# The opening of a fused Mamba-2 and expert-merge kernel: first decays in eight rows, a new order of loads, copies and products, and two stores on another queue

## The chip, the cores and the metric

The kernel runs on one core of one Trainium2 chip. The metric is device time in microseconds (us) of one execution. The five engines are TensorE (PE), VectorE (DVE), ScalarE (ACT), GpSimd (POOL) and SyncE (SP, which issues transfers). Each engine takes its instructions in the order in which the program gives them; between engines, semaphores make one wait for another. ACT and POOL can issue transfers too, and then the transfer stands in that engine's order.

## What is computed

First a Mamba-2 scan over 4 sequences of 768 steps, 8 heads, head width 32, state width 16. Then a merge of four expert networks over the 3072 tokens of width 256:

```python
la  = np.log(np.clip(a, 1e-06, 1.0))          # decays, per head and step
cum = np.cumsum(la, axis=-1)                  # inside a chunk
L   = np.exp(cum[:, :, :, None] - cum[:, :, None, :]) * causal
y   = (C B^T * L) x  +  (C state) * exp(cum)  # inside the chunk, and carried in
state = exp(sum la) * state + sum_j B_j x_j exp(cum_end - cum_j)

p = probs / (probs.sum(-1, keepdims=True) + 1e-09)
for e in range(4):
    out += p[:, e:e + 1] * (np.maximum(y @ w1[e], 0.0) @ w2[e])
```

All of it is in 32-bit floats. The two products with w1 (256 x 1024) and w2 (1024 x 256) for each expert are nearly all of the work.

## The kernel before

The 3072 tokens are 24 chunks of 128. The scan is done in 12 steps ("p") of two half chunks of 64, four sequences at once; the merge is done in four blocks of six chunks, with weights in pieces of 256 columns (`fb`), and with sums of pieces formed beforehand so that fewer products are needed. Two kinds of order occur.

The opening is written out by hand, lines 560 to 784. It loads the first decays, heads and tokens, makes the first step of the scan, and prepares what all later steps use. Everything after it is put in order by a planner (`Plan`, lines 69 to 273). It keeps a clock for each engine, gives every operation a home for its result and an engine where there is a choice (sums of weights or of token values may go to VectorE or GpSimd), and starts from two numbers, `now, START = 9.6, 11.0`: the times, in its own units, at which VectorE is free and PE begins the long run of products. Its order is fixed when the program is built.

In the opening these names matter:

- `a_q`, `a_q2`: the decays of step 0 (and 1), and of step 2, each 4 groups of heads by 2 halves of sequences. They lie in a tile of 128 rows, of which only eight hold data: row 32q + s, for group q and half s. The other rows are zero-filled first (lines 566, 567, 586), since the product that follows reads 32 rows of each group. `load_a` brings the data, `ready` clips it and zeroes the first column, and `spread` copies one row to 64 rows of a bank by a product with `own`, a 0/1 column: for each group q two products of 32 rows by 64 columns, one for each half s, in different corners of the array.
- `scan` (line 507) forms on VectorE the running products of the decays in `MT[0]`, for one group q of heads from `four[q]`, a bank of PSUM.
- `pr`, the expert probabilities; three small GpSimd sums make `total_p` (lines 623 to 626), VectorE takes its reciprocal, GpSimd forms `pc`, PE transposes it (`turn_gates`), ScalarE keeps it as `p_sb`, and `spread_gate` spreads the first expert's row to all rows, for `gate`.
- `mask` and `score`: heads B and C, masked by ScalarE and multiplied by PE into `seven`, four banks, in two halves s of the sequences.
- `end_of(q)`: a small GpSimd copy of the last columns of `MT[0]`, made before `masked(q)` (VectorE) or `aside(q)` (ScalarE and GpSimd, for q = 2) multiplies the scores into `MT[0]` in place. `F` is formed from these copies on GpSimd.
- `inner`: 64 small products of `MT[0]` with the tokens. Their result is copied to `yT0`, the first tokens of the merge. `state` makes the first state.
- `a_sb` (also called `cum`): all decays, loaded at once; clipped, logarithm on ScalarE, transposed (`turn_logs`), summed (`sum_logs`, `minus_logs`), and stored in memory (`cum_d`, `cumh_d`), from where later steps read them again (`ah`, `ab`). `p_d` holds the gates in the same way.
- `idle`: products of ones, whose result nobody reads, that keep PE running.

The loads go out on two queues. SP: half of the first decays, half of the heads, half of the tokens, all decays, two pieces of w1, the decays of step 2, two pieces of w1, the tokens of step 1, four pieces of w2. ACT: the probabilities, then the other halves. Eight transfers can be under way; the ninth waits for the landing of the first, and so on.

At the end, six pieces of the output are turned by PE, copied by VectorE or ScalarE, and stored by `send`, each by one transfer from SP and one from ACT (line 1395).

Of the kernel before, what the change touches and what calls it, by code (L numbers as in the profile page):

```python
# [8 lines left out]
FP32 = mybir.dt.float32  # L9
AF = mybir.ActivationFunctionType  # L10
ALU = mybir.AluOpType

P = 128
# [346 lines left out]
def kernel(  # L360
# [198 lines left out]

    a_q, a_q2 = (homes["V"][-i].rearrange("p c (t x) -> p c t x", t=NT) for i in (1, 4))  # L560

# [22 lines left out]
    tmask = const.tile([P, NT], FP32)  # L584
    nc.vector.memset(tmask, 0.0)
    nc.vector.memset(a_q2, 0.0)
    for fb in range(2):
        load_w1(fb, homes["W"][fb])
    for s in range(2):
        load_a(1, s, a_q2, nc.sync)  # L590
    for fb in range(2, 4):
        load_w1(fb, homes["W"][fb])
    for c in range(2):
        load_tokens(1, c, xt[1][:])
    for fb in range(4):
        load_w2(fb, homes["W"][4 + fb])

    ident = const.tile([P, P], FP32)
    make_identity(nc, ident)
# [19 lines left out]

    ready(a_q, 0)  # L620

# [14 lines left out]

    def turn_gates(banks):
        for z in range(NSEQ):
            nc.tensor.transpose(
                banks[z // 2][:rows, FB + z % 2 * P:FB + z % 2 * P + P],  # L640
                pc[:, z].rearrange("p e k -> p (e k)"), ident)
        for i in range(2):
            nc.scalar.copy(
                out=p_sb[:, :, 2 * i:2 * i + 2].rearrange("p e z i -> p z e i"),
                in_=banks[i][:rows, FB:].rearrange("p (z e i) -> p z e i", z=2, e=2))

    def spread_gate(bank, gate):
        nc.tensor.matmul(  # L648
            out=bank[:, FB:], lhsT=ident[:rows, 0:1].to_broadcast([rows, P]),
            rhs=p_sb[:, 0].rearrange("p z i -> p (z i)"), start=True, stop=True,  # L650
            skip_group_check=True)
        nc.scalar.copy(
            out=gate[:, :2].rearrange("p c x -> p (c x)"), in_=bank[:, FB:])

    def spread(a_q, e, banks, half, order=range(NQ)):
        for q in order:
            for s in range(2):
                k = slice(32 * q, 32 * q + 32)
                nc.tensor.matmul(  # L659
                    out=banks[q][HALF * s:HALF * s + HALF, FB * half:FB * half + FB].rearrange(  # L660
                        "p (x i) -> p x i", x=4),
                    lhsT=own[k, s].to_broadcast([32, HALF]),
                    rhs=a_q.rearrange("p c t x -> p (c t) x")[k, :, HALF * e:HALF * e + HALF],
                    start=True, stop=True, tile_position=(32 * q, HALF * s), skip_group_check=True)

# [27 lines left out]
    def turn_logs(bank):  # L693
        nc.scalar.activation(out=a_sb, in_=a_sb, func=AF.Ln)
# [45 lines left out]
    for i, q in enumerate(ORDER):  # L740
        scan(0, q, MT[0], four[q], 0)
        if not i:
            nc.vector.reciprocal(total_p, total_p)
    nc.gpsimd.tensor_mul(
        pc.rearrange("p z e k -> p z k e"), pr.rearrange("p (z k) e -> p z k e", z=NSEQ),
        total_p.rearrange("p (z k) e -> p z k e", z=NSEQ).to_broadcast([P, NSEQ, NC, E]))
    turn_gates(As)
    for s in range(2):
# [27 lines left out]
    sum_logs(As[0])  # L776
    nc.sync.dma_start(out=p_d, in_=p_sb)
    state(F[0], xt[0], As, 0, True)
    spread(a_q2, 0, four, 0, ORDER)
    minus_logs(ys[0])  # L780
    keep_state(homes["A"][0], As, 0)
    bound = const.tile([P, HALF], FP32)
# [7 lines left out]
    B512, B256 = {"DVE": D512, "POOL": 1.3}, {"DVE": D256, "POOL": .72}  # L790
    now, START = 9.6, 11.0

# [20 lines left out]
    yT[0, 0] = plan.taken("V", NV - 3, START)  # L813
    for i in (0, NV - 4, NV - 1):
        plan.homes["V"][i].free = now
# [560 lines left out]
    def last(k, groups):  # L1376
# [16 lines left out]
        def send(d, n, r, to):  # L1393
            for c, (queue, on_) in enumerate(((nc.sync, "SP"), (nc.scalar, "ACT"))):
                plan.add({on_: ISSUE}, lambda e, c=c, queue=queue: queue.dma_start(
                    out=dst[d, 3 * k + n, c][:, to],
                    in_=r.t[HALF * c:HALF * c + HALF, 0, to.start * P:to.stop * P].rearrange(
                        "p (s m) -> p s m", m=P)), lag=LANDING + .2, kb=32 * (to.stop - to.start),
                    reads=[r])

# [269 lines left out]
```

## Time and profile before

| what | us |
|---|---|
| three timed runs | 613.78, 614.91 (median), 617.61 |
| the profiled execution's own time | 613.47 |
| span of the profiled execution | 611.7 |
| PE busy | 600.8 (98%) |
| DVE busy | 493.8 (81%) |
| ACT busy | 276.6 (45%) |
| POOL busy | 140.4 (23%) |
| chain that ended last: share of PE | 97%, of it line 985 91% |
| first product of line 985 starts | 17.74 |

The span runs from the first instruction of the program to the last event; the own time has some 1.7 us more around it. Line 985 is the product of 128x256 of the merge (`product`). A chain of waits is followed back from the last instruction: at each step to what released it. Since PE has 97% of that chain, the time is the sum of PE's work and of the few places where PE waits or runs at a lower clock.

### The profile page before, as it was taken

To read this page: it belongs to the slowest core of one execution; us is meant where nothing else is said; L and a number is where in the kernel's file an instruction comes from. 1 tells how busy PE (TensorE), PEld (TensorE's weight loads), DVE (VectorE), ACT (ScalarE), POOL (GpSimd) and SP (SyncE) were. 2 spreads that over 40 slices of the span, in tenths; PEclk is the share of its full clock that TensorE was granted. 3 is DMA by queue.
4 is the path that set the end of the run, shared out by engine and by line. 5 is a ranking of instruction groups with operands and counts; after the bars stand their busy time and mean duration, and the time that the engine had idled before them with its cause. 6 is when DMAs were issued, how large, how long until landed. Compare 5 with 4: busy or idle time off the path is not lost.

```text
span 611.7 us, 12256 instructions
## 1 busy us (share of the span) xinstructions
PE 600.8 (98%) x4530; PEld 516.8 (84%) x4530; DVE 493.8 (81%) x851; ACT 276.6 (45%) x624; POOL 140.4 (23%) x147
## 2 busy tenths in 40 slices
PE   7999999999999999999999999999999999999997
PEld 4777888888888888888888888878888888888886
DVE  4769999999999995786988988386785989576794
ACT  3247557674542626765243343434444242434440
POOL 5662656656510000367401000000000000000000
PEclk8999999999999999999999999999999999999999
DMA  7577568878623329773432415963242322964002
GB/s 216 141 223 221 185 206 264 245 235 293 224 90 111 83 33 349 211 225 138 137 87 71 123 31 146 304 198 105 70 132 68 111 71 35 339 220 137 1 1 53
DMA packets 99856, 93.78 MB, mean 153 GB/s; under 512 B 33500, under 2 KB 69052, under 8 KB 99796
## 3 DMA queue, kind: packets, MB, share of 16 engines
q1 hardware_dynamic: 98120, 92.04, 49.3%
q10 hardware_dynamic: 1676, 0.96, 0.6%
q8 instruction: 36, 0.59, 0.4%
q14 instruction: 24, 0.20, 0.1%
HBM read 72.79 MB, written 20.17 MB: 152 GB/s over the span
## 4 chain that ended last, share of the span: by engine, by line
PE 97%; DMA 1%; issue 0%; SPq 0%; DVE 0%; POOL 0%; ACT 0%; DVEq 0%; POOLq 0%
PE bank L985 91%; PE bank L532 2%; PE bank L499 1%; PE bank L918 1%; DMA cum<-in_a_dram 1%; PE bank L541 1%; PE bank L1455 0%; PE bank L1391 0%; PE bank L659 0%; SPq L442 0%; PE bank L648 0%; PE bank L685 0%; DVE bank L1143 0%; DVE v L1020 0%; SPq L447 0%
## 5 line engine op out<-in xcount | busy, mean ns | idle before, releaser
L985 PE MATMUL bank<-v,w 128*128 128x256 f32 x1876 | 435.1, 380 | 1.6 <-issue 0.8
L985 PEld LDWEIGHTS bank<-v,w 128*128 128x128 f32 x1876 | 354.7, 190 | 52.6 <-issue 1.7
L985 PE MATMUL bank<-Y,w 128*128 128x256 f32 x692 | 177.1, 380 | 0.0
L1012 DVE TENSOR_TENSOR v<-v,v 128x512 f32<-128x512 f32 x238 | 175.1, 757 | 1.7
L1285 ACT COPY v<-bank 128x512 f32<-128x512 f32 x120 | 70.4, 587 | 202.7 <-PE bank L985 199.0
L985 PEld LDWEIGHTS bank<-Y,w 128*128 128x128 f32 x692 | 130.6, 190 | 19.4 <-ACT v L994 0.9
L1020 DVE SCALAR_TENSOR_TENSOR v<-bank,gate 128x512 f32<-128x512 f32 x162 | 111.1, 686 | 42.4 <-PE bank L985 37.9
L1045 POOL TENSOR_TENSOR w<-w,w 128x512 f32<-128x512 f32 (+1 forms) x84 | 95.6, 1151 | 102.9 <-DVE v L1012 31.1
L999 ACT COPY bank<-v 128x512 f32<-128x512 f32 x141 | 81.6, 593 | 19.7 <-DVE v L1020 14.2
L1143 DVE TENSOR_TENSOR bank<-bank,v 128x512 f32<-128x512 f32 x92 | 62.6, 693 | 33.3 <-PE bank L985 22.8
L994 ACT COPY v<-bank 128x512 f32<-128x512 f32 x111 | 65.2, 587 | 53.2 <-PE bank L985 45.1
L515 ACT ACTIVATE MT<-ab,neg 128x64 f32<-128x64 f32 x144 | 37.4, 338 | 0.0
L1012 DVE TENSOR_TENSOR v<-bank,v 128x512 f32<-128x512 f32 x30 | 20.6, 686 | 9.3 <-PE bank L985 6.5
L1321 DVE TENSOR_TENSOR v<-v,v 128x256 f32<-128x256 f32 x65 | 24.5, 415 | 1.0 <-ACT v L1285 0.7
L1020 DVE SCALAR_TENSOR_TENSOR v<-v,gate 128x512 f32<-128x512 f32 x30 | 24.1, 804 | 0.4
L880 POOL TENSOR_TENSOR cts<-ctm,dec 128x512 f32<-128x512 f32 x11 | 14.0, 1270 | 36.0 <-DVE Y L1115 24.2
L937 ACT COPY v<-bank 64x256 f32<-64x256 f32 (+1 forms) x33 | 12.3, 373 | 20.1 <-PE bank L541 15.8
L1012 POOL TENSOR_TENSOR v<-v,v 128x512 f32<-128x512 f32 x12 | 15.2, 1270 | 16.4 <-DVE v L1012 10.0
L682 DVE TENSOR_TENSOR MT<-bank,MT 128x256 f32<-128x256 f32 x47 | 16.6, 411 | 2.4 <-POOL ends L673 2.4
L520 DVE TENSOR_TENSOR MT<-MT,bound 128x512 f32<-128x512 f32 x18 | 16.5, 932 | 0.0
L489 ACT ACTIVATE ctm<-bct,tmask 128x256 f32<-128x256 f32 (+1 forms) x26 | 11.3, 485 | 6.3 <-DMA bct<-in_xbc_dram 6.3
L532 PEld LDWEIGHTS bank<-MT,xt 64*32 64x32 f32 x768 | 9.8, 110 | 2.4 <-issue 2.0
(95 smaller groups left out, 180.9 us busy)
## 6 DMA issues: line engine op xcount, KB each, us to landing
w<-w_d SPq DMA_DIRECT2D x128, 256.0 KB
w<-in_w_dram SPq DMA_DIRECT2D x72, 256.0 KB
w_d<-w SPq DMA_DIRECT2D x64, 256.0 KB
gate<-p_d SPq DMA_DIRECT2D x15, 384.0 KB
ab<-cum_d SPq DMA_DIRECT2D x36, 128.0 KB
xt<-in_xbc_dram SPq DMA_DIRECT2D x46, 96.0 KB
bct<-in_xbc_dram SPq DMA_DIRECT2D x5, 512.0 KB
out_dram<-v SPq DMA_DIRECT2D x144, 16.0 KB
```

The costliest lines, as they stand in the source:

```text
L515: nc.scalar.activation(out=MT[:, q, c, t], in_=ab[:, c, h], func=AF.Exp, bias=neg[:, e, t, i:i + 1])
L532: nc.tensor.matmul(out=y[to:to + 32], lhsT=xt[k, c, h:h + D], rhs=MT[k, q, c, t], start=start, stop=True, tile_position=(HALF * s, to), sk ...
L682: nc.vector.tensor_mul(v, bank[:, FB * half:FB * half + FB], v)
L985: nc.tensor.matmul(out=o, lhsT=w[:, j], rhs=x if half is None else x[:, j], start=(start and j == 0), stop=(j == 1), skip_group_check=True)
L994: act(.5, lambda e: nc.scalar.copy(out=flat(v), in_=bank.t), reads=[bank], writes=[v])
L999: act(.54 if to - lo > FB else .32, lambda e: nc.scalar.copy(out=bank.t[:, lo:to], in_=flat(v)[:, lo:to]), reads=[v], writes=[bank])
L1012: plan.add(engines, lambda e: (on(e).tensor_add if sign > 0 else on(e).tensor_sub)(flat(v), whole(x), whole(y)), reads=[x, y], writes=[v], ...
L1020: dve(D512, lambda e: nc.vector.scalar_tensor_tensor(out=h.t, in0=whole(x).rearrange("p (j m) -> p j m", j=JJ), scalar=0.0, in1=g.t[:, 2 * ...
L1045: (on(e).tensor_add if sign > 0 else on(e).tensor_sub)(out, x, y)
L1143: dve(D512, lambda e: (nc.vector.tensor_add if sign > 0 else nc.vector.tensor_sub)(to.t, bank.t, whole(x)), reads=[x, bank], writes=[to])
L1285: act(.5, lambda e: nc.scalar.copy(out=flat(v), in_=bank.t), reads=[bank], writes=[v], hold=HOLD)
L1321: plan.add(engines, lambda e: (on(e).tensor_add if sign > 0 else on(e).tensor_sub)(o[1](), x[1](), y[1]()), reads=[v for v in vs if v is n ...
```

## The change

The first decays now lie in rows 0 to 7 of their tile (row 4s + q), and nothing is filled with zeros. `own` becomes a table of 8 rows, with a 0/1 block for each group, in a free tile, and `spread` is one product of 8 rows by 128 columns for each group. Both halves of `a_q` are made ready at once. The loads are ordered anew: the probabilities go out on ACT after the decays and the heads, all tokens go on SP, the decays of step 2 on ACT, and of w2 two pieces only; the other two follow the stores of the sums. GpSimd's copies `ends` come before its other work, two of them ahead of `pc`; the clip of `a_sb` goes to VectorE after the masks, its logarithm to ScalarE after that. `turn_gates` writes one bank and stands between the two halves of the scores. Of the second spread of `a_q`, two groups stand after the scores and two after `inner`; `spread_gate` uses a bank of `four`; `state` moves ahead of the sums of logs. One `idle` of 256 columns becomes one of 128, and two of 128 go. The planner starts from 9.2 and 10.8, and one more tile is held until `now`. The two stores of output piece (0, 0) go out from GpSimd.

```diff
-    a_q, a_q2 = (homes["V"][-i].rearrange("p c (t x) -> p c t x", t=NT) for i in (1, 4))
+    ROWS = 2 * NQ
+    a_q, a_q2 = (homes["V"][-i][:ROWS].rearrange("p c (t x) -> p c t x", t=NT) for i in (1, 4))
...
-    nc.vector.memset(a_q[:, 0], 0.0)
-    nc.gpsimd.memset(a_q[:, 1], 0.0)
-    nc.scalar.dma_start(out=pr, in_=probs)
...
-            out=a_q.rearrange("(q r) c t x -> q r c (t x)", q=NQ)[:, s], in_=a_rows[k, s])
+            out=a_q[NQ * s:NQ * s + NQ].rearrange("q c t x -> q c (t x)"), in_=a_rows[k, s])
     for s, queue in enumerate((nc.sync, nc.scalar)):
         load_a(0, s, a_q, queue)
-    load_heads(0, bct[0], slice(0, 2))
-    load_heads(0, bct[0], slice(2, 4), nc.scalar)
-    load_tokens(0, 0, xt[0][:])
-    load_tokens(0, 1, xt[0][:], nc.scalar)
+        load_heads(0, bct[0], slice(2 * s, 2 * s + 2), queue)
+    nc.scalar.dma_start(out=pr, in_=probs)
     nc.scalar.preload_act_table_set("natural_log_exp_and_others")
+    for c in range(2):
+        load_tokens(0, c, xt[0][:])
+    for s in range(2):
+        load_a(1, s, a_q2, nc.scalar)
...
-    nc.vector.memset(a_q2, 0.0)
-    for fb in range(2):
-        load_w1(fb, homes["W"][fb])
-    for s in range(2):
-        load_a(1, s, a_q2, nc.sync)
-    for fb in range(2, 4):
+    for fb in range(4):
         load_w1(fb, homes["W"][fb])
...
-    for fb in range(4):
+    for fb in range(2):
         load_w2(fb, homes["W"][4 + fb])
...
-    own = const.tile([P, 2, 1], FP32)
-    nc.vector.reduce_sum(
-        own, ident.rearrange("p (q r) -> p r q", r=32)[:, 0:2], axis=mybir.AxisListType.X)
+    own = homes["V"][-5][:ROWS].rearrange("p a (q s j) -> p (a q) s j", s=2, j=HALF)
+    nc.vector.tensor_copy(
+        out=own, in_=ident[:ROWS, :ROWS].rearrange("p (s q) -> p q s", s=2).unsqueeze(3).to_broadcast(
+            [ROWS, NQ, 2, HALF]))
...
-    ready(a_q, 0)
+    for e in range(2):
+        ready(a_q, e)
...
+    def spread(a_q, e, banks, half, order):
         for q in order:
...
+            nc.tensor.matmul(
+                out=banks[q][:, FB * half:FB * half + FB].rearrange("p (x i) -> p x i", x=4),
+                lhsT=own[:, q].rearrange("p s j -> p (s j)"),
+                rhs=a_q.rearrange("p c t x -> p (c t) x")[:, :, HALF * e:HALF * e + HALF],
+                start=True, stop=True, skip_group_check=True)
...
     idle(BANK[6], 0, 4)
-    idle(BANK[7], 0, 2)
+    idle(BANK[7], 0, 1)
     spread(a_q, 0, four, 0, ORDER)
-    idle(BANK[7], 0, 1)
     idle(BANK[7], 0, 1)
...
-        if not i:
+        if q == 3:
             nc.vector.reciprocal(total_p, total_p)
+    for q in ORDER[:2]:
+        end_of(q)
     nc.gpsimd.tensor_mul(
...
-    turn_gates(As)
-    for s in range(2):
-        score(0, ctm[0], bct[0], seven, 0, s)
-    clip(nc.gpsimd, a_sb)
-    for q in ORDER:
+    for q in ORDER[2:]:
         end_of(q)
+    score(0, ctm[0], bct[0], seven, 0, 0)
+    turn_gates(four[2])
+    score(0, ctm[0], bct[0], seven, 0, 1)
     aside(2, seven[2])
+    keep_gates(four[2])
+    spread(a_q, 1, four, 1, (3, 0))
     for q in (3, 0, 1):
         masked(q, MT[0], seven[q])
-    spread_gate(ys[1], homes["gate"][0])
-    idle(four[0], 2, 3)
-    ready(a_q, 1)
+    clip(nc.vector, a_sb)
+    nc.scalar.activation(out=a_sb, in_=a_sb, func=AF.Ln)
+    spread_gate(four[2], homes["gate"][0])
...
-    turn_logs(As[1])
+    spread(a_q, 1, four, 1, (1, 2))
...
-    spread(a_q, 1, four, 1, ORDER)
-    sum_logs(As[0])
-    nc.sync.dma_start(out=p_d, in_=p_sb)
     state(F[0], xt[0], As, 0, True)
+    turn_logs(As[1])
     spread(a_q2, 0, four, 0, ORDER)
-    minus_logs(ys[0])
+    sum_logs(As[0])
+    nc.sync.dma_start(out=p_d, in_=p_sb)
+    for fb in range(2, 4):
+        load_w2(fb, homes["W"][4 + fb])
     keep_state(homes["A"][0], As, 0)
+    minus_logs(ys[0])
...
-    now, START = 9.6, 11.0
+    now, START = 9.2, 10.8
...
-            for c, (queue, on_) in enumerate(((nc.sync, "SP"), (nc.scalar, "ACT"))):
+            by = ((nc.sync, "SP"), (nc.scalar, "ACT")) if (d, n) != (0, 0) else ((nc.gpsimd, "POOL"),) * 2
+            for c, (queue, on_) in enumerate(by):
```

In this diff `keep_gates` is the second half of the old `turn_gates`: one copy of 24x512 from the bank to `p_sb` on ScalarE.

More of the change, by code (lines that the diff above doesn't have):

```diff
@@ L572, in load_a @@
         queue.dma_start(
-            out=a_q.rearrange("(q r) c t x -> q r c (t x)", q=NQ)[:, s], in_=a_rows[k, s])
+            out=a_q[NQ * s:NQ * s + NQ].rearrange("q c t x -> q c (t x)"), in_=a_rows[k, s])
     for s, queue in enumerate((nc.sync, nc.scalar)):
         load_a(0, s, a_q, queue)
-    load_heads(0, bct[0], slice(0, 2))
-    load_heads(0, bct[0], slice(2, 4), nc.scalar)
-    load_tokens(0, 0, xt[0][:])
-    load_tokens(0, 1, xt[0][:], nc.scalar)
+        load_heads(0, bct[0], slice(2 * s, 2 * s + 2), queue)
+    nc.scalar.dma_start(out=pr, in_=probs)
     nc.scalar.preload_act_table_set("natural_log_exp_and_others")
+    for c in range(2):
+        load_tokens(0, c, xt[0][:])
+    for s in range(2):
+        load_a(1, s, a_q2, nc.scalar)
     nc.sync.dma_start(
         out=a_sb, in_=a.rearrange("c h s -> (c h) s").rearrange("(p r) s -> p r s", r=2))
-    tmask = const.tile([P, NT], FP32)
-    nc.vector.memset(tmask, 0.0)
-    nc.vector.memset(a_q2, 0.0)
-    for fb in range(2):
-        load_w1(fb, homes["W"][fb])
-    for s in range(2):
-        load_a(1, s, a_q2, nc.sync)
-    for fb in range(2, 4):
+    for fb in range(4):
         load_w1(fb, homes["W"][fb])
@@ L594 @@
         load_tokens(1, c, xt[1][:])
-    for fb in range(4):
+    for fb in range(2):
         load_w2(fb, homes["W"][4 + fb])
+    tmask = const.tile([P, NT], FP32)
+    nc.vector.memset(tmask, 0.0)
     ident = const.tile([P, P], FP32)
@@ L635, with turn_gates, keep_gates @@
     p_sb = homes["V"][0][:rows].rearrange("p e (z i) -> p e z i", z=NSEQ)
-    def turn_gates(banks):
+    def turn_gates(bank):
         for z in range(NSEQ):
             nc.tensor.transpose(
[L640 to L645, printed above, removed]
+                bank[:rows, z * P:z * P + P], pc[:, z].rearrange("p e k -> p (e k)"), ident)
+    def keep_gates(bank):
+        nc.scalar.copy(
+            out=p_sb.rearrange("p e z i -> p z e i"),
+            in_=bank[:rows].rearrange("p (z e i) -> p z e i", z=NSEQ, e=2))
     def spread_gate(bank, gate):
         nc.tensor.matmul(
-            out=bank[:, FB:], lhsT=ident[:rows, 0:1].to_broadcast([rows, P]),
+            out=bank[:, :FB], lhsT=ident[:rows, 0:1].to_broadcast([rows, P]),
             rhs=p_sb[:, 0].rearrange("p z i -> p (z i)"), start=True, stop=True,
@@ L652, in spread_gate @@
         nc.scalar.copy(
-            out=gate[:, :2].rearrange("p c x -> p (c x)"), in_=bank[:, FB:])
-    def spread(a_q, e, banks, half, order=range(NQ)):
+            out=gate[:, :2].rearrange("p c x -> p (c x)"), in_=bank[:, :FB])
+    def spread(a_q, e, banks, half, order):
         for q in order:
-            for s in range(2):
[L658 to L664, printed above, removed]
+            nc.tensor.matmul(
[3 more added lines that the diff above has]
+                start=True, stop=True, skip_group_check=True)
     MT, F = homes["MT"], homes["F"]
@@ L693, in turn_logs @@
     def turn_logs(bank):
-        nc.scalar.activation(out=a_sb, in_=a_sb, func=AF.Ln)
         for t in range(NT):
@@ L739 @@
         mask(0, ctm[0], bct[0], slice(2 * s, 2 * s + 2))
-    for i, q in enumerate(ORDER):
+    for q in ORDER:
         scan(0, q, MT[0], four[q], 0)
-        if not i:
+        if q == 3:
             nc.vector.reciprocal(total_p, total_p)
+    for q in ORDER[:2]:
+        end_of(q)
     nc.gpsimd.tensor_mul(
@@ L746 @@
         total_p.rearrange("p (z k) e -> p z k e", z=NSEQ).to_broadcast([P, NSEQ, NC, E]))
-    turn_gates(As)
-    for s in range(2):
-        score(0, ctm[0], bct[0], seven, 0, s)
-    clip(nc.gpsimd, a_sb)
-    for q in ORDER:
+    for q in ORDER[2:]:
         end_of(q)
+    score(0, ctm[0], bct[0], seven, 0, 0)
+    turn_gates(four[2])
+    score(0, ctm[0], bct[0], seven, 0, 1)
     aside(2, seven[2])
+    keep_gates(four[2])
+    spread(a_q, 1, four, 1, (3, 0))
     for q in (3, 0, 1):
         masked(q, MT[0], seven[q])
-    spread_gate(ys[1], homes["gate"][0])
-    idle(four[0], 2, 3)
-    ready(a_q, 1)
+    clip(nc.vector, a_sb)
+    nc.scalar.activation(out=a_sb, in_=a_sb, func=AF.Ln)
+    spread_gate(four[2], homes["gate"][0])
     for c in range(2):
@@ L774 @@
     ready(a_q2, 0)
-    spread(a_q, 1, four, 1, ORDER)
+    state(F[0], xt[0], As, 0, True)
+    turn_logs(As[1])
+    spread(a_q2, 0, four, 0, ORDER)
     sum_logs(As[0])
     nc.sync.dma_start(out=p_d, in_=p_sb)
-    state(F[0], xt[0], As, 0, True)
-    spread(a_q2, 0, four, 0, ORDER)
+    for fb in range(2, 4):
+        load_w2(fb, homes["W"][4 + fb])
+    keep_state(homes["A"][0], As, 0)
     minus_logs(ys[0])
-    keep_state(homes["A"][0], As, 0)
     bound = const.tile([P, HALF], FP32)
@@ L813 @@
     yT[0, 0] = plan.taken("V", NV - 3, START)
-    for i in (0, NV - 4, NV - 1):
+    for i in (0, NV - 5, NV - 4, NV - 1):
         plan.homes["V"][i].free = now
@@ L1398, in send @@
                         "p (s m) -> p s m", m=P)), lag=LANDING + .2, kb=32 * (to.stop - to.start),
-                    reads=[r])
+                    reads=[r], port=False)
         def piece(d, n, x, y, sign):
```

## The prediction

> **What bounds the kernel.** I read the page first: TensorE (PE) is busy 600.8 of the 611.7 us span and the granted clock is full in all but the first of its 40 slices, so a change pays only where PE stands still or runs slowly. I then asked for busy time by stretches, and for the chain of waits in order of time. From 17.73 us, where the long run of 128x256 products (L985) begins, to 594 us PE is busy 574.66 of 576.27 us. The rest lies in the opening and in the last 10 us, and both are touched by this change.
>
> ```profile
> 4.02 4.23 DMA cum<-in_a_dram
> ...
> 8.33 0.48 POOL cum L613
> ...
> 9.46 0.32 POOL ends L673 x2
> ...
> 9.81 0.43 DVE MT L682
> ...
> 11.79 2.32 PE bank L532 x64
> ```
>
> Each row of the chain is start, time, what. The load of all decays (`cum`) holds GpSimd's clip, the clip stands in front of GpSimd's small copies `ends`, and VectorE may not mask `MT` in place before `ends` has read it. So PE stands still from 8.27 to 10.29 us. The 64 products of `inner` then take 2.32 us; the same 64 later take about 0.8 (the chain has "0.72 PE bank L532 x49" at 30.07). The stretches say why:
>
> ```profile
> 3.92:7.33 3.41, 1.98 (x25) 1.12 (x25) 2.54 (x6) 3.01 (x7) 0.88 (x4) 1.00 1.04 302
> 7.33:10.75 3.42, 1.41 (x34) 0.92 (x34) 1.05 (x4) 0.55 (x2) 2.36 (x7) 1.00 0.99 285
> 10.75:14.16 3.41, 3.41 (x69) 2.77 (x68) 0.53 (x3) 0.69 (x2) 3.01 (x7) 0.50 0.90 264
> ...
> 57.00:200.00 143.00, 142.98 (x1255) 123.78 (x1256) 141.19 (x225) 80.14 (x210) 68.09 (x58) 1.00 0.66 206
> ```
>
> Columns: stretch, its length, busy time of PE, weight load, VectorE (DVE), ScalarE (ACT), GpSimd (POOL), then the granted clock. After 3.42 us with only 1.41 us of PE work the clock is 0.50 for 3.41 us; after 1.98 us of work it stayed full.
>
> **The opening, part by part.** These rows of the timeline (start, time, engine, line) price it:
>
> ```profile
> 2.67 0.26 POOL L623 TENSOR_TENSOR pairs<-pr 128x48 f32<-128x48 f32 x1 [0.25 <-DMA pr<-in_probs_dram]
> ...
> 4.09 0.69 PE L659 MATMUL bank<-v,own 32*64 32x256 f32 x16 [0.35 <-POOL upto L628]
> ...
> 4.85 0.69 DVE L507 TENSOR_TENSOR_SCAN MT<-bank,identr 128x256 f32<-128x256 f32 x1 [0.85 <-PE bank L659]
> ...
> 6.23 0.61 PE L639 MATMUL bank<-ident,pc 128*24 128x128 f32 x4 [0.81 <-POOL pc L744]
> ```
>
> *Zero fills.* The two loads of the first decays were issued at 1.29 and 1.32, behind two memsets that end at 1.20; the first transfer of ACT's queue went out at 0.81. So the loads move 0.48 us forward, and with them the clip (3.57 to 3.09) and the spread (4.09 to 3.6). The warm-up products, 2.90 us in all, lose two of 128x256 for two of 128x128 (0.63 to 0.37 each) and end near 3.2, in time. The third fill was beside other work.
>
> *Full-height products.* One call of 128x256 is two matmuls, and 28 of these in L985 took 6.21 us, 0.222 each; four calls cost 1.78 us where sixteen small ones took 0.69, so 1.09 more for each of three spreads. No row has a product of eight rows; its bounds are 0.69 and 1.78, and I take 1.78, the rows with as many columns. A scan needs only its own call (0.44 us), so the first comes about 0.75 us after the spread's start, as before: 4.35. The second ends at 5.6.
>
> *Probabilities behind the heads.* This part works against the change. `pr` was ACT's first transfer: issued 0.81, landed 2.60. Now ACT issues the decays (1.15 us), half of the heads (0.40), then `pr`, at 2.45. Alone it took 1.79 us, giving 4.25; `cum` took 4.23 from its issue, giving 6.7. The trace's landing times put the heads of ACT's queue 3.77 us after their issue (2.50 to 6.27), so now about 5.77. `pr` follows them on that queue; I take 5.9. GpSimd waits for it in order: from 2.67 its three sums took 0.94 us, and the `upto` block 0.96. The reciprocal now stands on VectorE between the second and third scan; it waits for the sums until 6.9 and holds the other two scans, which end at 8.45 where they ended at 7.44. `ends` of two groups run 7.9 to 8.2, `pc` to 8.55, the rest of `ends` to 8.85. PE does the first half of the scores at about 5.7 (its masks need heads landed at 4.8), then waits with `turn_gates` (0.61) for `pc`; the second half of the scores, 0.49, is queued behind it and ends at 9.6.
>
> *After the scores.* Masking starts at 9.65 instead of 9.81 and ends at 10.75 (1.09). ScalarE copies the third group (0.37), then the gates (two copies took 0.61) until 10.65; meanwhile PE spreads two groups (0.87) at no cost. Gate spread 0.44, to 11.15. `inner`, 0.8 at full clock, to 12.0. One spread call, to 12.45. The next waits for the gate's copy, which waits for clip (0.41 on VectorE, after the masks), Ln (0.42) and copy (0.37): 12.05, hidden. It also needs `cum`, now issued behind four token transfers at about 4.7, so landed by 8.95; needed at 10.75. If that cover went, each us of it would hold PE. Then the second call 12.9, `state` 13.35 (0.46), `turn_logs` 13.65, four spread calls 15.4, the two sums of logs about 0.5 each. Products begin at 16.4 instead of 17.73: **-1.3 us at full clock**.
>
> *Clock.* PE now rests in one piece, 6.15 to 8.6, longer than the 2.02 us of before. If the 3.41 us stretches lie as in this profile, the one from 7.33 holds some 2.0 us of work and stays full. Where a stretch begins between 4.75 and 6.6 it holds 1.41 or less, and half clock follows; between 4.2 and 7.2 less than 1.98, undecided. That is 54% to 88% of phases, if the phase varies; the same count for before gives about the same. Half clock over 3.41 us of dense work costs up to 1.7; I take half of that for an average, 0.85, and so **-0.5 us** for the opening against this profile, between -1.3 and +0.4.
>
> *After the opening.* Two loads of `w2` now stand behind the sums' stores on SP: 1.07 us of issue at about 18.2, ahead of the `ah` loads, which then start at 19.3 instead of 18.56. `cts` follows on GpSimd near 26; PE wants it 11.1 us after its first product, at 27.5, so 1.3 us are left. The order of the built programs shows eight 512-wide sums and two fades moved from GpSimd to VectorE, 6.8 us by 0.757 and 0.35; all come after a third of PE's calls, past 200 us, where VectorE was busy 306.36 of 394 us. Cost nothing.
>
> **The end.** Rows of the timeline:
>
> ```profile
> 606.40 1.46 SPq L1395 DMA_DIRECT2D out_dram<-v  x2
> 606.41 0.71 ACTq L1395 DMA_DIRECT2D out_dram<-v  x1
> 607.16 0.37 ACT L1408 COPY v<-bank 128x256 f32<-128x256 f32 x1 [0.56 <-issue]
> ```
>
> Two stores leave SP and ACT for GpSimd's queue. ACT's copy at 607.16 waited for that issue and starts at 606.61; SP has one store less, and its last issue ends at 608.8 instead of 609.47; the span ended 2.2 us after it. -0.67. No row has a store issued by GpSimd. Each could be as short as SP's 0.60 or as long as GpSimd's largest operation, 1.27: out at 607.6 to 608.95. I take **-0.5**.
>
> Sum: -0.5 - 0.5 = -1.0 on the profiled execution's 613.47 us (611.7 and 1.7 around it). That run lies 1.4 below the median of 614.91, whose runs reach 617.61; on the median the forecast is 613.9, and between the two I say **613.7**.
>
> **Rivals.**
>
> *The wait only changes its owner, and the clock halves (slower).* If `pr` lands at 6.7, all of the chain behind it is 0.8 later, PE rests 3.2 us, and the half clock lies on `inner`: -1.3 + 0.8 + 1.7 = +1.2, with the end +0.7: 614.2 on the own time, 615.6 on the median. For it: the 1.41 us row, and PE's in-order queue with half the scores behind `pc`. Against: with the stretches as in the profile 1.98 us stayed full. It decides where PE rests over 2.0 us of one stretch. [...] Chance 0.27.
>
> *Everything is uncovered (faster).* `pr` lands at 4.25: then `pc` is ready by 6.9, masking starts near 8, products at 14.7, -3.0; with the end -3.5: 611.4 on the median. For it: its 1.79 us alone. Against: the heads ahead of it on the same queue. Chance 0.14.
>
> *The middle stalls.* 57 to 200 us had 141.19 of 143 us of VectorE busy. If the new order puts even the moved 6.8 us there, 1.8 us fit and 5.0 delay PE: about 619. Against: the order above. Chance 0.06, half of it past 1%.
>
> *GpSimd's stores end last.* It decides where each takes over 1.2 us; at 2.4 each they are out at 611.2, +2.4: 616.8. Chance 0.05.
>
> **How the numbers follow.** The forecast (-0.3 to -2.2 on either base) has 0.48. About 1% (6 us) is what a measurement of this kernel can tell. Nothing but the stall, or a better middle that no row shows, reaches it: faster 0.03, within 0.93, slower 0.04. The range takes the uncovered case below and the slower one with the scatter of the runs above: 610.6 to 617.4.
>
> **What would show it.** Right: `pairs` waits on `pr` until about 5.9, reciprocal near 6.9, `turn_gates` near 8.6, `inner` at 11.2, first L985 between 16.4 and 17.9, SP's last store 0.7 us sooner after the last copy, no new PE rest after that. Wrong: `pr` before 5; PE resting on Ln or `cum`; products beginning after 18.5; more than 3 us of rest between the first product and the last ten us.

## The result, and the profile after

The changed kernel takes 623.35 us (median of 4 executions, 622.62 to 623.55), the kernel before beside it 614.72 (4 executions, 613.78 to 617.61): a ratio of 1.013 with a 95% interval of 1.0096 to 1.0165. It is slower by 8.6 us, outside the forecast range.

The profiled execution took 623.45 us, with a span of 621.7 against 611.7. I set the start of the same pieces of work in the two traces side by side:

| piece of work | before, us | after, us | late by |
|---|---|---|---|
| first of the long products (L985; L982 after) | 17.74 | 24.70 | 6.97 |
| first `outputs` (L918; L915 after) | 29.41 | 37.89 | 8.48 |
| a long product matched by its place in the order | 83.45 | 91.58 | 8.13 |
| another, behind VectorE's densest stretch | 123.19 | 132.85 | 9.66 |
| first turned piece of the end | 600.67 | 610.54 | 9.87 |
| end of the span | 611.74 | 621.74 | 10.00 |

So 8.5 us are lost in the first 38 us, another 1.2 net by 133 us, and the end neither gives nor takes anything that counts. The busy times and the clock, from the page of after:

```profile
PE 614.0 (99%) x4502; PEld 526.4 (85%) x4502; DVE 497.1 (80%) x860; ACT 277.1 (45%) x623; POOL 128.2 (21%) x137
...
PEclk9999999999999999999999999999999999999999
```

TensorE is busy 13.2 us longer than before with 28 instructions fewer. At full clock the three new spreads should account for some 3.3 us of it (1.09 each by the prediction); the rest is work that runs slower. The clock row shows nothing of it, and misleads here. The first record of the clock in this trace is a step to full at 28.41 us, and the page prints the 28.41 us ahead of it as full. The durations say what it was. The chain of waits of after (start, time, what):

```profile
0.85 2.47 PE bank L679 x4
3.32 3.71 PE bank L654 x8
...
7.75 1.06 PE bank L499 x16
8.81 0.96 PE bank L636 x4
9.77 1.06 PE bank L499 x16
10.83 2.00 PE bank L654 x4
...
13.69 2.32 PE bank L532 x64
...
19.12 3.71 PE bank L654 x8
...
24.77 8.92 PE bank L982 x32
```

L654 is the new spread: eight matmuls in 3.71 us are 0.464 each, where a 128x256 matmul at full clock took 0.222 before. The 64 products of `inner` (L532) take 2.32 us, the figure that they had in the half-clock stretch of before. And at 19.12 the spread still takes 3.71: the whole opening runs at half clock, and the first long products with it (nine matmuls from 24.70 in 4.02 us, 0.447 each). The opening up to the start of the long products, in the busy times by stretches (columns as there: stretch, length, PE, weight load, VectorE, ScalarE, GpSimd, clock):

```profile
3.92:17.73 13.81, 13.81 (x120) 9.40 (x118) 4.76 (x12) 3.39 (x9) 6.08 (x19) 1.00 0.63 191
17.73:24.70 6.97, 6.97 (x55) 4.66 (x54) 2.76 (x4) 0.69 (x2) 0.00 (x0) 1.00 0.00 0
```

TensorE is busy for all of these 20.8 us. Nothing that it waits for is left in the opening; it is slow. The transfers and sums came about when they were forecast, in the timeline of after (start, time, engine, line, and in brackets the idle time ahead and its releaser):

```profile
5.94 0.27 POOL L620 TENSOR_TENSOR pairs<-pr 128x48 f32<-128x48 f32 x1 [3.50 <-DMA pr<-in_probs_dram]
...
6.92 0.30 DVE L735 RECIPROCAL total_p<-total_p 128x24 f32<-128x24 f32 x1 [0.87 <-POOL total_p L623]
...
8.74 1.03 PE L636 MATMUL bank<-ident,pc 128*24 128x128 f32 x4
```

`pr` lands at 5.94 (forecast 5.9), the reciprocal runs at 6.92 (6.9), the turn of the gates at 8.74 (8.6). What else is new, in TensorE's waits of after (waiting line, releaser: sum, times, longest):

```profile
PE bank L982 <- DVE v L1017: 1.7, 2, 1.3
```

These two waits, 0.35 us at 58.9 and 1.31 at 116.7, stand against one of 0.82 us at 39.8 before.

### The profile page after: what moved, and what is told of

It reads as the page before. It is cut to its first block, busy times and chain, and to the rows that moved or that the text cites. A ratio compares the mean times of both kernels' runs of the same rounds, so it can differ in the third digit from the quotient of the medians.

```text
span 621.7 us, 12182 instructions
## 1 busy us (share of the span) xinstructions
PE 614.0 (99%) x4502; PEld 526.4 (85%) x4502; DVE 497.1 (80%) x860; ACT 277.1 (45%) x623; POOL 128.2 (21%) x137
## 4 chain that ended last, share of the span: by engine, by line
PE 89%; DVE 8%; issue 1%; ACT 0%; DMA 0%; SPq 0%; POOL 0%; POOLq 0%; DVEq 0%
PE bank L982 82%; DVE v L1017 2%; PE bank L654 2%; DVE v L1009 2%; PE bank L532 2%; DVE MT L520 1%; PE bank L499 1%; DVE bank L1140 1%; PE bank L915 1%; DVE F L524 1%; PE bank L541 1%; DVE v L1533 1%; PE bank L679 1%; DVE MT L676 0%; DMA ah<-cumh_d 0%
## 5 line engine op out<-in xcount | busy, mean ns | idle before, releaser
L982 PE MATMUL bank<-v,w 128*128 128x256 f32 x1876 | 437.0, 381 | 2.4 <-DVE v L1017 1.7
L982 PEld LDWEIGHTS bank<-v,w 128*128 128x128 f32 x1876 | 356.1, 191 | 54.1 <-DVE v L1017 2.7
L1009 DVE TENSOR_TENSOR v<-v,v 128x512 f32<-128x512 f32 x244 | 178.7, 754 | 2.7 <-ACT v L991 1.0
L982 PE MATMUL bank<-Y,w 128*128 128x256 f32 x692 | 177.2, 380 | 0.0
L982 PEld LDWEIGHTS bank<-Y,w 128*128 128x128 f32 x692 | 130.5, 190 | 19.4 <-ACT v L991 0.9
L1042 POOL TENSOR_TENSOR w<-w,w 128x512 f32<-128x512 f32 (+1 forms) x82 | 91.0, 1118 | 105.8 <-DMA ab<-cum_d 29.6
L1393 POOL DMA_DIRECT2D out_dram<-v x2 | 1.4, 712 | 261.6 <-DVE v L1406 261.6
L507 DVE TENSOR_TENSOR_SCAN MT<-bank,identr 128x256 f32<-128x256 f32 x12 | 8.0, 678 | 5.3 <-PE bank L654 5.1
```

What stands on the lines that cost most here:

```text
L982: nc.tensor.matmul(out=o, lhsT=w[:, j], rhs=x if half is None else x[:, j], start=(start and j == 0), stop=(j == 1), skip_group_check=True)
L1009: plan.add(engines, lambda e: (on(e).tensor_add if sign > 0 else on(e).tensor_sub)(flat(v), whole(x), whole(y)), reads=[x, y], writes=[v], ...
L1042: (on(e).tensor_add if sign > 0 else on(e).tensor_sub)(out, x, y)
```

## The experiments

**The theories.** *Rows*: what opens the clock is not that TensorE is busy, but how much of the array its products use; products over 8 rows hardly count, so the clock stays half until the long products come. *Order*: it is the shorter warm-up and the new order, whatever the rows. For the rest: the plan's new numbers, the store queue, the place of the probabilities. Times are medians; ratios are against the kernel before, timed beside each run on its chip, with 95% intervals.

**e1_burst: the changed kernel with the warm-up products of before ahead of and behind the first spread.**

```
-    idle(BANK[7], 0, 1)
+    idle(BANK[7], 0, 2)
     spread(a_q, 0, four, 0, ORDER)
+    idle(BANK[7], 0, 1)
```

> The changed kernel with the idle products of before put back around the first spread (256 columns ahead of it, two of 128 behind it), nothing else. Theory 'rows' (the clock is granted for how much of the array is in use, and products of 8 rows hardly count): full clock for a stretch at most, then half again through the 8-row spreads; first 128x256 products at 19 to 24 us; 618 to 623 us. Rival 'burst' (only the shorter warm-up keeps the clock from opening): full clock from about 4 us on, first products near 16.5, 612 to 615 us.

622.99 us, ratio 1.0104 (1.0070 to 1.0138), 10 executions in two groups: four at 617.5 to 618.0 and six at 623.0 to 624.2. More warm-up doesn't cure it; the rival 'burst' had expected 612 to 615. In the profiled execution, one of the early group, the records show full clock from 12.04 to 18.86, half to 22.28 and full from there.

**e2_rows128: the changed kernel with its spread over all 128 rows.** The eight rows stay where they are, rows 8 to 127 are zero in the decays and in the table `own`, so the sums are the same.

```
+    nc.vector.memset(full_q[:, 0], 0.0)
+    nc.gpsimd.memset(full_q[:, 1], 0.0)
+    nc.vector.memset(full_q2, 0.0)
...
-    own = homes["V"][-5][:ROWS].rearrange(...)
+    own = homes["V"][-5].rearrange(...)
...
-    spread(a_q, 0, four, 0, ORDER)
+    spread(full_q, 0, four, 0, ORDER)
...
```

> The changed kernel with its spread products over 128 rows (data in rows 0 to 7 as before, the others zero-filled, in table and decays), same idle products, same columns, same count of products. Theory 'rows': full clock by about 7 us and kept, first 128x256 products at 16 to 18 us, 613 to 616 us. Rival 'burst': half clock until the long run as in the changed kernel, first products near 25, 623 us. A third, 'order' (the new order starves the array): also 623.

615.06 us, ratio 1.0001 (0.9984 to 1.0018): 8.3 us faster than the changed kernel, from 120 more rows that hold only zeros. All ten executions (614.24 to 616.11) lie below all four of the changed kernel. The clock is full from 7.41 us and stays so. TensorE in the timeline of e2_rows128:

```profile
3.62 3.75 PE L658 MATMUL bank<-v,v 128*128 128x256 f32 x8 [0.30 <-DVE v L618]
...
11.71 1.42 PE L532 MATMUL bank<-MT,xt 64*32 64x64 f32 x64
...
14.72 1.92 PE L658 MATMUL bank<-v,v 128*128 128x256 f32 x8
...
17.50 7.17 PE L986 MATMUL bank<-v,w 128*128 128x256 f32 x32
```

The first spread runs at half clock as in the changed kernel, 3.75 us. But behind it `inner` takes 1.42 instead of 2.32, a later spread 1.92 instead of 3.71, and the long products begin at 17.50 instead of 24.70.

**f4_rows32 and g4_rows64: the same with 32 and with 64 rows.**

```
-    full_q, full_q2 = (homes["V"][-i].rearrange(...
+    full_q, full_q2 = (homes["V"][-i][:64].rearrange(...
...
-    own = homes["V"][-5].rearrange(...
+    own = homes["V"][-5][:64].rearrange(...
```

> The 128-row version with 32 rows in its spread products, the other 24 of them zero. Theory 'rows' in its form 'the share of rows in use is what counts': between the two, half clock for a part of the opening, 617 to 623 us. In its form 'one group of 32 rows is enough': as with 128 rows, 615. If zeros in the data were what counted, 128 rows and 8 rows would have been alike; they were not.

> The kernel of e2_rows128 with the spread's products over 64 rows instead of 128 (e2_rows128 gave 615.06 and the full clock from 7.41 us; f4_rows32 gave 622.43 and the full clock lost again until 21.17 us; the 8 rows of the change gave 623.35). Theory share of rows: the clock follows the share of the array's rows in use, so 64 rows lie between: either they are enough (614.3 to 616) or they are not (616 to 622 and a full clock that is lost again). Rival threshold at all rows: only products over 128 rows count, and 64 rows give what 32 gave, 621.5 to 623.5.

32 rows: 622.43 us, ratio 1.0093 (1.0063 to 1.0124). 64 rows: 622.55 us, ratio 1.0083 (1.0048 to 1.0119). Neither is enough, and the two can't be told apart, as the rival with a threshold at all rows had forecast (621.5 to 623.5 for 64 rows). Both have two groups again, four of ten executions at 616.0 to 617.2 and six at 622.3 to 624.1. The profiled execution of g4_rows64, of its late group, in the timeline:

```profile
14.41 2.39 PE L532 MATMUL bank<-MT,xt 64*32 64x64 f32 x64
...
19.84 3.78 PE L658 MATMUL bank<-v,v 64*128 64x256 f32 x8
...
25.49 2.93 PE L986 MATMUL bank<-v,w 128*128 128x256 f32 x6
```

Half clock to the end of the opening, as in the changed kernel; the first record of full clock is at 29.93. So in this opening 64 rows did not bring full clock before 29.93 us in the profiled execution, and 128 brought it at 7.41 in that of e2_rows128.

**h1_form8: the kernel before, with only the form of the spread changed.** Order, warm-up products, loads and stores are those of before; with the form go the zero fills and the place of the table `own`, for which the plan holds one more tile until `now`.

```
-            for s in range(2):
-                    lhsT=own[k, s].to_broadcast([32, HALF]), ... tile_position=(32 * q, HALF * s)
+                lhsT=own[:, q].rearrange("p s j -> p (s j)"),
+                rhs=a_q.rearrange("p c t x -> p (c t) x")[:, :, HALF * e:HALF * e + HALF],
...
-    nc.vector.memset(a_q[:, 0], 0.0)
```

> The kernel before, with nothing changed but the form of the spread: the decays in eight rows with no zero fills, and one product of 8 rows by 128 columns per bank in place of two of 32 rows by 64 columns side by side; the order of the opening, its warm-up products, its loads and the stores are those of before. Theory rows: these 24 products no longer count for the clock, which is half for most of the opening: 618 to 623, with the first long product after 20 us. Rival order: it was the order and the shorter warm-up of the changed kernel, and this form alone keeps the time of before, 614 to 616, with the first long product by 18.5 us.

620.62 us, ratio 1.0097 (1.0072 to 1.0122); all four executions, 618.63 to 623.2, lie above the 16 of before timed beside them (613.84 to 618.08; another 35 of before on that chip reached 620.15). The form alone costs 6.0 us, with before's full warm-up and before's order. TensorE in its timeline:

```profile
3.67 3.78 PE L656 MATMUL bank<-v,v 8*128 8x256 f32 x8
...
13.67 2.39 PE L532 MATMUL bank<-MT,xt 64*32 64x64 f32 x64
...
24.69 3.54 PE L981 MATMUL bank<-v,w 128*128 128x256 f32 x10
```

Its records have full clock from 16.74 to 20.15 us and then from 26.98. Not all of the 6.0 us is a matter of when the clock opens, and here the traces show something more. The opening of before doesn't always have full clock early either. The run f1_stores (below) differs from before only in two stores at the very end, and in its profiled execution (615.19 us) the first record of full clock is at 17.23 us, where the profile of before has it at 3.94. Its timeline:

```profile
15.16 1.16 PE L659 MATMUL bank<-v,own 32*64 32x256 f32 x16
...
19.43 7.17 PE L985 MATMUL bank<-v,w 128*128 128x256 f32 x32
```

With half clock until 17.23, the old opening reaches the long products at 19.43, 1.7 us later than in the profile of before; the changed one, at half clock throughout, reaches them at 24.70. A new spread takes 3.78 us at half clock in the timeline, an old one 1.16. So in these profiles two things come with the new form: half clock lasts longer (the last of it in the opening ends at 26.98 us in h1_form8 and 28.41 in the changed kernel, at 14.18 in before and 17.23 in f1_stores), and the products that run at it are over three times as long.

**e3_idle8 and e4_cut: the kernel before with its warm-up products over 8 rows, and with the changed kernel's shorter warm-up.**

```
-            lhsT=one.to_broadcast([P, P]), rhs=one.unsqueeze(1).to_broadcast([P, to - lo, P])
+            lhsT=one[:8].to_broadcast([8, P]), rhs=one[:8].unsqueeze(1).to_broadcast([8, to - lo, P])
```

```
-    idle(BANK[7], 0, 2)
-    spread(a_q, 0, four, 0, ORDER)
     idle(BANK[7], 0, 1)
+    spread(a_q, 0, four, 0, ORDER)
...
-    idle(four[0], 2, 3)
```

> The kernel before with its idle products over 8 rows instead of 128, same columns and count. Theory 'rows': no full clock near 4 us; the opening runs at half clock for longer, first 128x256 products at 19 to 25 us, 617 to 623 us. Rival 'burst' or any theory in which busy time counts whatever the rows: as before, 614 to 617 us.

> The kernel before with the shorter idle products of the change (128 columns ahead of the first spread, one of 128 behind it, none before the inner products). Theory 'rows': the packed spreads use all 128 rows, so most executions open as before, 613 to 617 us. Rival 'burst': the clock does not open early, 619 us or more.

e3_idle8: 616.52 us, ratio 1.0033 (1.0003 to 1.0063): five executions at 614.3 to 615.2, five at 617.9 to 620.1. The median lies where the rival had it (614 to 617) and not where *rows* did. In the profiled execution (620.13) the clock first opens at 21.62 us and the long products begin at 20.62 instead of 17.74. But TensorE also rests there for 2.89 us at 43.14, ahead of a long product, where before rests 0.82 at 39.77, and the records have half clock again from 45.51 to 48.92. So this run doesn't show what 8 rows in the warm-up products alone cost. e4_cut: 614.98 us, ratio 1.0003 (0.9985 to 1.0021), so the shorter warm-up by itself costs nothing that can be measured in the median. Its profiled execution (616.97) opened late as well: full clock from 22.08, long products at 20.73. With h1_form8, which keeps the whole warm-up and the order of before, this takes the ground from *order*.

**f1_stores and f2_spact: the stores alone.** f1_stores is the kernel before with only the two stores of the last pieces moved to GpSimd; f2_spact is e2_rows128 with them back on SP and ACT, the same edit backwards.

```
+            by = ((nc.sync, "SP"), (nc.scalar, "ACT")) if (d, n) != (0, 0) else ((nc.gpsimd, "POOL"),) * 2
+            for c, (queue, on_) in enumerate(by):
-                    reads=[r])
+                    reads=[r], port=False)
```

> The kernel before with the change's last part alone: the two stores of output piece (0, 0) issued by GpSimd. From the last turned pieces to the end of the span the kernel before took 11.07 us and the changed one 11.20. Theory 'lands late': GpSimd's stores are issued in time but land about 3.7 us after, so the gain on SP and ACT is eaten; 11.1 to 11.3 us, time within 0.4 us of before. Rival (my forecast): 10.5 us, time 0.5 us less than before.

> The 128-row version (e2_rows128) with these two stores back on SP and ACT. 'Lands late': the same as e2_rows128 within 0.4 us, 615. My forecast of the end: 0.5 us more, 615.5.

f1_stores: 615.01 us, ratio 0.9992 (0.9968 to 1.0015). f2_spact: 614.91 us, 1.0002 (0.9986 to 1.0018), against 1.0001 with the stores on GpSimd. No gain and no loss; the 0.5 us that I had forecast for either is not there. The end of f1_stores' chain of waits:

```profile
607.73 0.44 DVE v L1409
608.16 0.30 issue
608.47 0.85 POOL out_dram L1396
609.31 0.60 POOLq L1667
```

From the end of the copy on VectorE that these stores wait for, 608.17, the two issues on GpSimd take until 609.91, and the span ends at 613.4: 10.97 us from the first turned piece, where before has 11.07. SP's last issue does end 1.02 us sooner, counted from the first turned piece (7.78 and 8.80). But GpSimd's stores are not what lands last, as the theory had it: the last packet of GpSimd's queue ends at 611.40, those of SP and ACT at 611.67 and 611.77. Why the shorter queues gain only 0.1 us stays open.

**f3_probs: f2_spact with the probabilities first on ACT's queue again.**

```
+    nc.scalar.dma_start(out=pr, in_=probs)
...
-    nc.scalar.dma_start(out=pr, in_=probs)
```

> As f2_spact, and the load of the probabilities first on ACT's queue again. In e2_rows128 GpSimd waited for it until 6.5 us, the reciprocal stood on VectorE at 7.46 in front of two scans, and PE's gate transposes began at 8.89. Theory 'probabilities behind the heads cost': that wait is gone, the second half of the scores no longer waits for it, first 128x256 products 1 to 2.5 us sooner (15 to 16.5), time 613 to 614. Rival 'next wait': masks or the scans hold the scores just as long, less than 0.5 us gained.

613.96 us, ratio 0.9976 (0.9958 to 0.9994), 0.95 us below f2_spact; the long products begin at 16.66 (f2_spact: 17.40), a little after the forecast range. Its timeline:

```profile
2.83 0.26 POOL L624 TENSOR_TENSOR pairs<-pr 128x48 f32<-128x48 f32 x1 [0.40 <-DMA pr<-in_probs_dram]
...
8.06 0.61 PE L640 MATMUL bank<-ident,pc 128*24 128x128 f32 x4
```

The sums run at 2.83 instead of 6.40 (f2_spact), and the turn of the gates no longer waits for `pc`; in f2_spact it waited 1.20 us. The wait that the change had made was real, and about 1 us under a full clock.

**g1_plan and g2_burst: f3_probs with the plan's two numbers of before, and f3_probs with a second warm-up product.**

```
-    now, START = 9.2, 10.8
+    now, START = 9.6, 11.0
```

```
-    idle(BANK[7], 0, 1)
+    idle(BANK[7], 0, 2)
     spread(full_q, 0, four, 0, ORDER)
```

> The kernel of f3_probs with only the two numbers of the plan put back (now 9.6 and START 11.0 in place of 9.2 and 10.8). Theory plan: the waits of TensorE on VectorE's gating at 49.6 us (1.00 us) and 107.7 us (1.22 us) in f3_probs come from the order that the planner writes with the earlier start, so they shrink to what before has (0.82 us in one wait) and the time falls by about 1 us, to 612.6 to 613.4. Rival places: the waits come from the tiles of V and W that hold other things in the opening, and the two numbers move nothing that matters: the same waits within 0.3 us and 613.5 to 614.5.

> The kernel of f3_probs with two products of ones, 128x512, ahead of the first spread instead of one. Theory clock: the first of them runs at half clock, so the second adds up to 0.4 us of TensorE work at full rows before the spread; the full clock is recorded up to 1 us sooner (6.98 us in f3_probs), the spread of the first four products ends no later than there, and the time is 613.3 to 614.0. Rival delay: the decays are ready by then, the spread starts 0.2 to 0.4 us later and everything behind it with it: 614.1 to 614.6.

g1_plan: 611.35 us (610.97 to 612.06), ratio 0.9945 (0.9932 to 0.9958): faster than before, and 2.6 us below f3_probs, more than I expected. g2_burst: 612.89 us, 0.9968 (0.9956 to 0.9980), 1.07 below f3_probs, a little better than expected. TensorE's waits of f3_probs, and then of g1_plan:

```profile
PE bank L986 <- DVE v L1021: 2.2, 2, 1.2
...
PE bank L986 <- DVE Y L1116: 0.2, 1, 0.2
```

```profile
PE bank L986 <- DVE bank L1144: 1.0, 2, 0.7
```

The waits on the gating (L1021) and on `Y`, 2.4 us, are gone; the other group grew from 0.7 to 1.0. With 0.33 us of earlier first products that makes 2.4 of the 2.9 us by which the profiled spans differ; where the other 0.45 came from I did not find.

**i1_afterplan and i2_both: the same two numbers in the changed kernel itself, and g1_plan with the second warm-up product.** The edits are those above.

> The changed kernel with only the two numbers of its plan put back (now 9.6 and START 11.0). In the changed kernel TensorE waits twice on VectorE's gating, 1.7 us in all, 1.3 of it at 117 us. Theory plan: these waits go as they did in g1_plan, the half clock of the opening stays, and the time falls by 1 to 2.6 us: 620.7 to 622.4. Rival clock alone: with the opening 7 to 8 us late in any case the plan's start makes no difference here, the waits stay within 0.4 us and the time is 622.6 to 624.

> g1_plan and g2_burst together: the spread over 128 rows, stores on SyncE and ScalarE, probabilities first on ScalarE's queue, the plan numbers of before and two products of ones ahead of the first spread. If the two gains are independent (611.35 and a further 1.07, by which g2_burst stood below f3_probs) it is 610.0 to 610.8; if the earlier end of the opening is eaten by the next wait (VectorE's gating, which the plan now covers from a start of 11.0) it is 611.0 to 611.8.

i1_afterplan: 620.70 us, ratio 1.0062 (1.0033 to 1.0091), 2.65 below the changed kernel. Its waits on the gating are gone too. That execution opened early, but so did the profiled one of f4_rows32 (long products at 19.29 and 19.67), which has the new numbers and still waits twice, 1.7 us in all; so the plan's numbers make the waits and not the late opening. The stretch in which VectorE is densest, first of the changed kernel, then of i1_afterplan:

```profile
62.00:120.00 58.00, 56.62 (x614) 47.98 (x613) 57.63 (x95) 34.71 (x101) 28.16 (x25) 1.00 0.70 216
```

```profile
62.00:120.00 58.00, 57.92 (x623) 49.34 (x622) 57.17 (x95) 35.48 (x104) 36.42 (x31) 1.00 0.70 215
```

GpSimd (the fifth busy time) does 8.3 us more in this stretch with before's numbers (i1_afterplan is some 5 us further on in its work here); VectorE has 0.83 us to spare instead of 0.37, and TensorE is held 0.08 us instead of 1.38. Over the span GpSimd works 140.5 us with before's numbers (before: 140.4) and 128.2 with the new ones.

i1_afterplan has two groups as well, four executions at 615.2 to 615.4 and eight at 620.5 to 621.4. Its profiled execution is of the early group, and has the order of the opening that the changed kernel has. That allows a comparison of one opening under two clocks. Its stretches:

```profile
13.94:17.35 3.41, 3.41 (x47) 2.29 (x46) 1.92 (x5) 0.52 (x2) 1.33 (x2) 1.00 0.27 64
17.35:20.77 3.42, 3.42 (x17) 2.65 (x17) 1.93 (x5) 1.49 (x6) 0.00 (x0) 0.50 0.20 49
```

The records have full clock from 10.53 to 17.35. In the stretch from 13.94 TensorE is busy for all of it, with products of 8, 64 and 96 rows, and the clock is 0.50 right behind it. In the profile of before TensorE was busy for 1.98 of the 3.41 us from 3.92, the clock was still 1.00 in the 3.42 us behind them, and that work was warm-up products and the gates' turn over 128 rows, and the old spread, which fills four bands of 32 rows.

i2_both: 611.28 us, ratio 0.9944 (0.9923 to 0.9965). It can't be told from g1_plan: the second warm-up product's gain is eaten once the waits in the middle are gone.

## Why the prediction was wrong

**The step that failed: the clock.** The prediction counted busy time. It held that a stretch with some 2.0 us of work stays full, that at worst one stretch of 3.41 us is halved, "up to 1.7" us, and took 0.85. Of the 2.0 us it counted for the stretch from 7.33, 0.87 were two groups of the new products over 8 rows, counted like any other work. Measured: half clock up to 28.41 us, some eight times 3.41, and 8.3 us between the 8 rows and the 128 (623.35 and 615.06) with all else of the change in place. The price of the products went wrong with it: 1.09 us more for each of three spreads was worked out from matmuls at full clock (0.222 each). At half clock it is some 2.6 us (3.78 against 1.16), 7.9 in all and not 3.3, and TensorE had no rest left in the opening to hide them. The row that should have warned was in view: no row of the trace had a product of eight rows, and I bounded its duration from both sides but not what it does to the clock. TensorE was busy throughout from 3.92 to 24.70 us, six times the 3.41 us, and the clock did not open before 28.41; being busy, as the trace shows it, was not enough here.

**Right in part, and partly by luck.** The eight matmuls of a spread took 1.92 us in e2_rows128 at full clock, forecast 1.78. The spread started at 3.25 instead of 3.6, since the clip ran at 2.61 and not 3.09. `pr` at 5.94, reciprocal 6.92, turn of the gates 8.74: each within 0.15 us of its forecast. For `pr` this is luck: ACT issued it at 1.88 and not at 2.45, since the load of the decays ahead of it took 0.56 us to issue and not 1.15, and it then took 4.06 us to come and not 3.45; the two errors cancel. The reciprocal follows from it. The turn of the gates is luck too: `pc` was ready at 8.29, and what held the turn was the first half of the scores, at half clock until 8.8. Masking began at 11.00 instead of 9.65, since the gates' turn and the 16 scores behind it took 2.0 us at half clock where the forecast has 1.1. That the late probabilities cost time is confirmed by f3_probs (0.95 us); the prediction carried it inside its sum, without a figure of its own. With full clock from 7.41 us the long products began at 17.50 (e2_rows128) and not at 16.4; against before's 17.74 the opening is worth 0.24 us and not 1.3. Here the gate's turn still waited for `pc` until 8.89, and `inner`, forecast at 11.2, began at 11.71 and took 1.42 instead of 0.8.

**The moved sums: mis-sized.** The prediction costed the eight sums and two fades moved from GpSimd to VectorE at nothing, because they all stand behind 200 us in the built order. That reading was wrong: up to 200 us GpSimd runs three of the sums and both fades fewer in the trace of after (64 and 3 sums against 66 and 4, no fades against 2), and between 57 and 200 us VectorE had only 1.8 us to spare by the prediction's own count. What it cost is told by putting the two numbers back: 2.6 us at full clock (g1_plan against f3_probs), 2.65 in the changed kernel (i1_afterplan). The rival of the middle stalls had the mechanism, VectorE full between 57 and 200 us, and too large a size; it was a second cause beside the clock and not the one that decided.

**The end: mis-sized.** The forecast was -0.67 from SP's shorter queue, and -0.5 after a share for GpSimd. The last issue did come sooner (f1_stores), and the end of the span didn't follow it: 10.97 us after the first turned piece against 11.07, ratio 0.9992 with an interval that holds 1. The assumption that the span ends a fixed 2.2 us after SP's last issue failed. The rival in which GpSimd takes over 1.2 us for each store fell too: 0.85 and 0.60.

**The rival on the other side.** "The wait only changes its owner, and the clock halves" named the clock, for a reason that was not it: TensorE rested nowhere in the opening. Its price for the half clock, 1.7 us, was a fifth of what came (8.3).

**What stays open.** How the clock counts was not shown: whether by rows, by rows times columns or by something else that zeros share, or how many rows between 64 (622.55 us) and 128 (615.06 us) would have been enough. Full rows alone don't settle it either. Records that follow one another in the opening lie 3.41 us apart or twice that (e1_burst: 12.04, 18.86, 22.28; h1_form8: 16.74, 20.15, 26.98); that the work in one such stretch decides the clock of the next is my assumption, and no run shows it. Reckoned back on it in steps of 3.41 us, the stretch ahead of the first full clock in before (0.53 to 3.94) held 2.90 us of warm-up products over 128 rows; in f1_stores, with the same products, such a stretch lay at 0.17 to 3.58 and held 2.73, and the clock stayed half until 17.23. Only four executions of the changed kernel were timed, all late; the runs with the nearest openings (e1_burst, i1_afterplan, f4_rows32, g4_rows64) have an early group some 6 us lower in four of ten or twelve, so the changed kernel probably has one too, and 8.6 us is the cost of its late group. Within the two openings, what came ahead of the full clock at 10.53 in i1_afterplan and was missing in the changed kernel can only be argued: the same reckoning places the stretch there at 7.11 to 10.53, with 0.65 us of the warm-up products over 128 rows and all of the gates' turn; in the changed kernel the stretches lie at 7.94 to 11.35, and the warm-up products, which end at 7.76, are outside.

## What to carry to other kernels

Before a product's shape is changed for fewer instructions, ask over how many rows it runs in the opening: in this kernel's, 120 rows of zeros were worth 8.3 us (623.35 against 615.06). The version with them, the old plan, the old stores and the probabilities first (g1_plan) beats the kernel before by 3.3 us and the changed one by 12.0. Price a longer product at half clock too, where it may have to run there (a spread over 8 rows: 3.78 us at half clock in after, 1.99 at full in i1_afterplan). Read the clock from the durations of a known form and not from the clock column, which says nothing ahead of its first record (in after it reads full up to 28.41 us, where eight matmuls of a spread took 3.71). And numbers that a planner starts from are part of the kernel: change them alone before believing that they follow from the rest.

## What the runs showed of the hardware that was not expected

- TensorE was busy for all of the 3.41 us from 13.94 to 17.35 in i1_afterplan, and the clock was 0.50 for the 3.42 us behind them; in the changed kernel it was busy for 20.8 us, 3.92 to 24.70, without full clock before 28.41. Most products were over 8 to 96 rows in both. With 120 rows of zeros more in each spread the clock was full from 7.41 us (e2_rows128).
- The first record of full clock has no fixed place. With one and the same opening it came at 3.94 us in before and at 17.23 in f1_stores, 13.29 us apart, which is no multiple of 3.41. The executions of one kernel fall in groups as well: i1_afterplan at 615.3 and 620.8, g4_rows64 at 616.2 and 622.6; the profiled one of i1_afterplan's early group had full clock from 10.53, that of g4_rows64's late group from 29.93. In the six versions with 128 rows, where it came by 7.41 us in the profiles, the executions of each lie within 1.9 us, against 4.2 us over 16 of before.
- At half clock eight matmuls of a spread took 3.78 us over 8 rows in the timeline (after), 3.75 over 32 (f4_rows32), 3.75 to 3.78 over 64 and 3.75 over 128 (e2_rows128): here the product's own time at half clock did not change with its rows.
